# RWKV attention and a squared-ReLU FFN: chunk scores cut to 64-token halves, bonus sums moved to TensorE

## The chip, the cores and the metric

One Trainium2 chip, one core. The metric is device time in microseconds of one execution of the whole kernel, with all loads from and stores to device memory. All tensors are float32.

## What is computed

For each of 4 batches and 8 heads (head size 48) a linear recurrence runs over 768 tokens; its output, heads side by side, goes through a two-layer FFN with a squared ReLU.

```python
# r, k, v, w: [4, 8, 768, 48];  u: [8, 48];  w_in: [384, 2048];  w_out: [2048, 384]
for t in range(S):
    cur = einsum('bhd,bhe->bhde', u * k[t], v[t])
    y[t] = einsum('bhd,bhde->bhe', r[t], state + cur)
    state = w[t][..., None] * state + einsum('bhd,bhe->bhde', k[t], v[t])
x = y as [4 * 768, 384]
h = maximum(x @ w_in, 0)
out = (h * h) @ w_out
```

## The kernel before

**Chunks and units.** The 768 tokens are cut into 6 chunks of C = 128. A *unit* is one chunk of one batch, all 8 heads: 24 units, 4 per chunk. The 8 heads are handled as 4 pairs; a pair's two heads lie in partitions 0 to 47 and 64 to 111 (J = 64, HP = 112), so that products of one head use a 64x64 quarter of the TensorE array and four of them can be under way at once. Tokens are also cut into two halves of Q = 64.

**A unit, step by step** (`attention(c, b, rank)`):
- load w, k, r token-major into `st` (two units at a time) and v into `vt`; for chunk 0 TensorE transposes `st` into `pt` (L618, through PSUM), later chunks do it with a 32x32 VectorE transpose (L581) and small DMAs;
- `scan` (L630): running product of w along the tokens; `ln` (L637, L638): its inverse by Ln and Exp on ScalarE; `rt` (L641) and `kn` (L647, L648, L653): r times the decay before it, k over the decay up to it;
- the bonus term: r x k x u on GpSimd (L660, L662), a VectorE reduce per head and three small moves that put each token half where its block needs it (L666 to L669), then `diag` (L680, ScalarE): the 64x64 diagonal times the sum, eight times;
- `far` (L682, L683): a check of w's range, which would lead to a slow path at the end (not taken with these inputs);
- `scores` (L693): k against r, for the first 64 keys against all 128 queries, for the second 64 against the last 64; `mask` (L696) copies the causal part over the diagonal tile `m`;
- `past` (L715): the state `S` before the chunk against r, plus four transposes of k (L720), moved by ScalarE (L739); `mix` (L728): v against `m`, accumulated onto past; `outer` (L747): k^T v, added to the state by VectorE (L809), which GpSimd multiplies with the chunk's decay `Ec` (L812);
- `x` (L789, L790): the result in two parts, high and low, for the FFN's split products; a fourth pair goes through `x3` and six small DMAs.

Scores take two PSUM banks of a pool "a", past and mix take two. In chunk 0 there is no state; there the fourth pair's result is placed by a selection product (L755).

**FFN.** Per chunk 16 steps f of 128 hidden columns (`ffn`): nine products of 512 (or, in the first steps of chunks 0 and 1, 256) columns into a bank `hp` (L832), ReLU on ScalarE (L837), times itself on VectorE (L838), high part on ScalarE (L840), low part on VectorE (L841), and per batch three products of 384 columns into `ob` (L847). Weights arrive as raw words and are split into high and low parts by ScalarE, VectorE and GpSimd (L532 to L553) during chunk 0.

**Order of work.** Every step is handed to a planner (`Plan`) with an engine, an assumed cost, what it reads and writes, and a rank from a hand-kept table (`Ranks`). The planner plays the steps through with these costs, engine by engine, and writes each engine's instructions in the order of the assumed start times. A `mode` marks steps in 64x64 tiles: it assumes a price for entering and leaving them. Pools have a fixed number of places, and a step waits for a free one:

```python
P.pool("hp", hps)    # 2 PSUM banks
P.pool("a", pas)     # 2 PSUM banks
P.pool("m", ...)     # 7 tiles [128, 512]
```

Up to 110 us of planned time it puts filler transposes of the identity (L888) where it expects TensorE to be idle.

## Time and profile before

| | us |
|---|---|
| runs, median of 3 (range) | 546.95 (545.52 to 547.07) |
| the profiled execution | 545.76 |
| its span, first to last instruction | 543.9 |
| TensorE busy | 526.4 |
| VectorE busy | 367.1 |
| ScalarE busy | 281.8 |
| GpSimd busy | 101.4 |

In the page a busy time is the union of an engine's instructions. PE is TensorE's products, PEld its weight loads, DVE VectorE, ACT ScalarE, POOL GpSimd, SP the queue that issues most DMAs. A line such as L847 names the source line. Rows of the order of time give start, length, and how many instructions were merged; products overlap, so the distance to the next row's start says more than the length. f32 products of the attention appear as two instructions per call. TensorE's granted clock was 0.996 of full speed on the mean.

### The profile page before, as it was taken

What the parts mean: (1) busy time and instruction counts of PE and PEld (TensorE: products, weight loads), DVE (VectorE), ACT (ScalarE), POOL (GpSimd) and SP (SyncE); (2) the same over time, 40 slices, a digit from 0 to 9 for tenths busy, and PEclk for the clock granted to TensorE, in tenths of its full rate; (3) what the DMA queues carried; (4) which work ended last, traced back from release to release, by engine and by line L of the source; (5) the groups of instructions that cost most, each with busy time, mean ns of one, the idle gap of its engine ahead of it and who ended that gap; (6) DMA issues with size and microseconds to landing.
All of it is one profiled execution on the core that took longest, in us unless ns stands there. A gap on an engine that the chain in (4) does not pass through costs nothing.

```text
span 543.9 us, 12917 instructions
## 1 busy us (share of the span) xinstructions
PE 526.4 (97%) x5047; PEld 465.7 (86%) x5047; DVE 367.1 (67%) x770; ACT 281.8 (52%) x730; POOL 101.4 (19%) x121
## 2 busy tenths in 40 slices
PE   8899989999999999999999999999999999999995
PEld 8788978878999889988888888889888989899894
DVE  6889899989969596498859597875653233433331
ACT  3668568486664747356465757526433222432321
POOL 5344543144303021030301203020000000000000
PEclk9999999999999999999999999999999999999998
DMA  9979988666483745747256565644002000000001
GB/s 161 175 183 227 244 173 195 151 109 136 93 151 72 138 91 101 140 92 134 48 97 122 101 125 117 129 91 84 1 6 68 16 1 1 29 32 0 1 1 61
DMA packets 222978, 53.01 MB, mean 97 GB/s; under 512 B 212672, under 2 KB 217792, under 8 KB 222912
## 3 DMA queue, kind: packets, MB, share of 16 engines
q1 hardware_dynamic: 220016, 50.75, 46.6%
q10 hardware_dynamic: 2896, 1.38, 1.0%
q8 instruction: 42, 0.69, 0.6%
q14 instruction: 24, 0.20, 0.1%
HBM read 31.65 MB, written 4.72 MB: 67 GB/s over the span
## 4 chain that ended last, share of the span: by engine, by line
PE 77%; DMA 10%; DVE 4%; ACT 3%; SPq 3%; issue 1%; POOL 0%; ACTq 0%; DVEq 0%
PE hp L832 33%; PE ob L847 32%; DMA ri<-in_moe_w_in_dram 4%; DMA v<-in_v_dram 3%; PE a L693 3%; PE a L728 3%; DMA st<-in_w_dram 2%; PE a L715 2%; SPq L572 2%; PE a L720 1%; PE a L747 1%; ACT m L680 1%; SPq L605 1%; DVE g L841 1%; DVE pt L630 1%
## 5 line engine op out<-in xcount | busy, mean ns | idle before, releaser
L847 PE MATMUL ob<-wo,g 128*128 128x384 f32 x1152 | 223.4, 340 | 1.4 <-DVE g L841 1.4
L832 PE MATMUL hp<-x,wi 128*128 128x512 f32 (+1 forms) x1062 | 219.9, 355 | 3.4 <-DVE g L841 3.2
L847 PEld LDWEIGHTS ob<-wo,g 128*128 128x128 f32 x1152 | 198.9, 188 | 7.7 <-DVE g L841 2.2
L832 PEld LDWEIGHTS hp<-x,wi 128*128 128x128 f32 x1062 | 173.1, 188 | 32.8 <-DVE g L841 6.8
L838 DVE SCALAR_TENSOR_TENSOR hp<-hp,t 128x512 f32<-128x512 f32 (+1 forms) x118 | 69.8, 593 | 91.3 <-ACT t L837 90.8
L837 ACT ACTIVATE t<-hp 128x512 f32<-128x512 f32 (+1 forms) x118 | 61.1, 518 | 118.5 <-PE hp L832 64.2
L841 DVE TENSOR_TENSOR g<-hp,g 128x512 fp32r<-128x512 f32 (+1 forms) x118 | 68.9, 585 | 32.3 <-ACT g L840 31.6
L840 ACT CAST g<-hp 128x512 fp32r<-128x512 f32 (+1 forms) x118 | 59.7, 506 | 51.9 <-DVE hp L838 51.5
L680 ACT ACTIVATE m<-diag,beta 128x64 f32<-128x64 f32 x192 | 50.0, 340 | 11.6 <-DVE beta L668 7.3
L660 POOL TENSOR_TENSOR st<-st 128x384 f32<-128x384 f32 x24 | 24.3, 1017 | 65.6 <-DVE st L581 58.4
L630 DVE TENSOR_TENSOR_SCAN pt<-pt,zero 112x128 f32<-112x128 f32 x80 | 29.0, 412 | 1.7 <-DMA st<-in_w_dram 1.7
L790 DVE SCALAR_TENSOR_TENSOR x<-a,x 112x128 fp32r<-112x128 f32 (+2 forms) x68 | 20.2, 329 | 12.2 <-ACT x L789 10.9
L696 DVE COPY_PREDICATED m<-caus,a 128x384 f32<-128x384 uint8 x48 | 25.9, 584 | 3.1 <-PE a L693 2.9
L662 POOL TENSOR_TENSOR st<-st,un 128x384 f32<-128x384 f32 x24 | 27.3, 1141 | 1.6
L581 DVE STREAM_TRANSPOSE st<-st 128x1152 f32<-128x1152 f32 x20 | 27.0, 1361 | 0.0
L728 PEld LDWEIGHTS a<-m,v 64*48 64x48 f32 (+1 forms) x768 | 20.5, 126 | 7.3 <-issue 4.1
L637 ACT ACTIVATE m<-pt 112x512 f32<-112x512 f32 x24 | 15.2, 631 | 22.3 <-DVE pt L630 19.4
L693 PEld LDWEIGHTS a<-pt 48*64 48x64 f32 x768 | 19.2, 133 | 7.8 <-ACT m L680 1.6
L789 ACT ACTIVATE x<-a 112x128 fp32r<-112x128 f32 (+2 forms) x68 | 18.1, 313 | 14.1 <-PE a L747 7.0
L728 PE MATMUL a<-m,v 64*48 64x64 f32 (+3 forms) x768 | 24.8, 250 | 0.4 <-DVE m L696 0.4
L693 PE MATMUL a<-pt 48*64 48x128 f32 (+1 forms) x768 | 22.8, 250 | 1.4 <-DVE pt L653 1.4
L812 POOL TENSOR_TENSOR S<-S,Ec 112x192 f32<-112x192 f32 x16 | 8.1, 508 | 82.8 <-DVE S L809 82.8
(86 smaller groups left out, 441.8 us busy)
## 6 DMA issues: line engine op xcount, KB each, us to landing
pt<-st SPq DMA_DIRECT2D x120, 96.0 KB, 2.3
ro<-in_moe_w_out_dram SPq DMA_DIRECT2D x8, 768.0 KB, 7.4
v<-in_v_dram SPq DMA_DIRECT2D x88, 48.0 KB, 2.5
st<-in_w_dram SPq DMA_DIRECT2D x11, 384.0 KB, 4.4
st<-in_k_dram SPq DMA_DIRECT2D x11, 384.0 KB, 5.7
st<-in_r_dram SPq DMA_DIRECT2D x11, 384.0 KB, 5.7
out_dram<-q SPq DMA_DIRECT2D x20, 192.0 KB, 2.1
ri<-in_moe_w_in_dram SPq DMA_DIRECT2D x8, 384.0 KB, 6.4
```

The costliest lines, as they stand in the source:

```text
L581: V.transpose(out=zt[:, i].rearrange("a t p q i -> a t (p q) i"), in_=sv[:, :, i].rearrange("s t p q x -> s t (p q) x"))
L630: lambda p=p: V.tensor_tensor_scan(out=pt[:, 0, p], data0=src(0)[:, p], data1=zero.broadcast_to([HP, C]), initial=1.0, op0=ALU.mult, op1=A ...
L662: P.add("pool", 0.97, rank("rk"), lambda: G.tensor_tensor(out=rk(), in0=rk(), in1=un.rearrange("s (h d) -> s h d", d=D), op=ALU.mult), w=[ ...
L680: A.activation(Ms[j].tile[:, mo(p, y):mo(p, y) + Q], diag2, AF.Copy, scale=beta.tile[:, i:i + 1])
L693: T.matmul(mts[j].tile[q * Q:q * Q + Q, o:o + C - y * Q], kq[js, g:g + Q], pt[js, 1, 2 * q + p, y * Q:], start=True, stop=True, skip_group ...
L728: T.matmul(spot(p)[to:to + n + D, y * Q:], vt.tile[qs, o - n:o + D], Ms[j].tile[qs, mo(p, y):mo(p, y) + C - y * Q], start=(c == 0 and p == ...
L832: T.matmul(hp.tile[:, 0:n], wi[f][:, wl, kt], xT[:, kt, xl, xs], start=(m == 0), stop=(m == 3 * KT - 1))
L837: P.add("act", 0.49 if full else 0.28, rank("g"), lambda: A.activation(t(), h(), AF.Relu), r=[hp], w=[(g, 1)])
L838: P.add("dve", 0.6 if full else 0.33, rank("g"), lambda: V.scalar_tensor_tensor(out=h(), in0=h(), scalar=0.0, in1=t(), op0=ALU.max, op1=AL ...
L840: P.add("act", 0.48 if full else 0.26, rank("g"), lambda: A.copy(out=hi(), in_=h()), r=[hp], w=[(g, 0)])
L841: P.add("dve", 0.6 if full else 0.33, rank("g"), lambda: V.tensor_tensor(out=lo(), in0=h(), in1=hi().bitcast(F32), op=ALU.subtract), r=[hp ...
L847: T.matmul(obs[b][:, 0:DM], g.tile[0][:, gl, o:o + C], wo[f][:, wl], start=(f == 0 and m == 0), stop=(f == NF - 1 and m == 2))
```

## The change

- **Halves (chunks 1 to 5).** Scores are computed within each 64-token half only. The first half's k^T v is added to the state before the chunk, which gives a second state `S1` at mid-chunk; past then multiplies the first half's queries with `S` and the second half's with `S1`. `S2` is the state after the chunk before the decay.
- **Order of the groups.** From chunk 2 on, `advance(a, z)` puts past of one unit and outer of the next into one TensorE step, and mix of the one and scores of the next into another. In chunk 1 the units take these steps singly. Both banks of pool "a" are one tile `ab` and are always taken together. Outer alternates the banks against the column halves (`q ^ j`).
- **k's transposes** become a step of their own outside the 64x64 mode, into an `hp` bank, with one ScalarE copy.
- **Bonus sums (chunks 0 and 1).** VectorE multiplies r and k head-major; four small TensorE products with `ut` (u laid out by head, loaded by four small DMAs with 4-byte elements) sum over the head; ScalarE puts them in place. GpSimd's two passes, the reduce and the moves go for these units. In chunk 0 r is copied out of PSUM by ScalarE first.
- **FFN of chunk 0.** h x h is made on ScalarE as a Square of the ReLU's output.
- Mask, x and state steps work on both banks at once; one "m" tile less; all ranks and a few assumed costs differ.

The core of the diff (the rank tables left out):

```diff
-    LANES, RUNS, SLACK, START = 8, 2300, 1.0, 3.6
+    LANES, RUNS, SLACK, START = 8, 2300, 1.0, 4.0
...
-    pas = [ps_a.tile([128, 512], F32, name=f"a{i}") for i in range(2)]
+    ab = ps_a.tile([128, 1024], F32, name="ab")
+    pas = [ab[:, i * 512:i * 512 + 512] for i in range(2)]
...
+    ut = at.tile([HP, 2, 4], F32, name="ut")
+    G.memset(ut, 0.0)
+    for j in range(2):
+        for p in range(2):
+            nc.scalar.dma_start(out=ut[j * J:j * J + D, p]..., in_=u...)
...
+        if c < 2:   # attention: bonus sums of the first two chunks
+            P.add("dve", 0.59, rank("rk"), lambda: V.tensor_tensor(out=Ms[0]..., in0=turned(pt[:, 1]), in1=turned(src(2)), op=ALU.mult), ...)
...
+            def betas():
+                for g in range(4):
+                    T.matmul(bp.tile[:, g * 4:g * 4 + 4], Ms[0].tile[0:HP, g * C:g * C + C], ut[:, g // 2], start=(g == 0), stop=True, ...)
+            P.add("pe", 0.5, rank("beta"), betas, r=[Ms[0]], w=[bp])
+            def place_betas():
+                for q in range(2):
+                    A.copy(out=beta.tile[qs, 0:H]..., in_=bp.tile[qs, 0:16]...)
...
+            def turned_k():
+                for i, g in enumerate(range(0, 4, 3 - ys)):
+                    T.matmul(kp.tile[:, i * HP:i * HP + HP], kq[:, g * C:g * C + C], ident[0:HP, 0:HP], is_transpose=True, ...)
+            P.add("pe", 0.2 * ys, rank("ktp"), turned_k, r=KK, w=[kp])
+            P.add("act", 0.03 + 0.2 * ys, rank("kt"), lambda: A.copy(out=Kt..., in_=kp...), r=[kp], w=[Kt])
...
+            def outer(alone):     # 16 products of 48 columns (8 in the last chunk)
+                ...
+                T.matmul(ab[j * J:j * J + n, (q ^ j) * 512 + p * 2 * C + C + y * J:...], Kt..., vt..., start=(alone and p == 0 and y == 0), ...)
+            def inter():          # past: two states, 16 products of 64 columns
+                for h, t in enumerate((lambda: Ss[b], lambda: S1.tile)):
+                    ...
+                    T.matmul(ab[to:to + n + D, p * 2 * C + h * Q:...], t()[js, o - n:o + D], pt[js, 1, p, h * Q:h * Q + Q], ...)
+            def scores():         # 16 products of 64 columns
+            def mix():            # 16 products of 64 columns
...
+            def after_outer():
+                P.add("dve", 0.27, rank("S"), lambda: V.tensor_tensor(out=sv(S1.tile), in0=zone(0, D)[0:HP], in1=sv(Ss[b]), op=ALU.add), ...)
+                if not last:
+                    P.add("dve", 0.27, rank("S"), lambda: V.tensor_tensor(out=sv(S2.tile, 0), in0=zone(J, D)[0:HP], in1=sv(S1.tile), op=ALU.add), ...)
...
+    def advance(a, z):
+        if a: fns += [a["inter"]]
+        if z: fns += [lambda: z["outer"](not a)]
+        P.add("pe", cost, ..., lambda: group(fns), w=["Y", "dS", "scores"] + AB, mode=1, ...)
+        ...
+        if a: then += [a["mix"]]
+        if z: then += [z["scores"]]
+        P.add("pe", cost, ..., lambda: group(then), w=... + AB, mode=1, ...)
...
+        if c == 0:            # ffn
+            P.add("act", 0.49 if full else 0.28, rank("g"), lambda: A.activation(h(), t(), AF.Square), r=[(g, 1)], w=[hp])
+        else:
+            P.add("dve", ..., lambda: V.scalar_tensor_tensor(out=h(), in0=h(), scalar=0.0, in1=t(), op0=ALU.max, op1=ALU.mult), ...)
...
+            if c == 1:
+                advance(a, None)
+                advance(None, z)
+            else:
+                advance(a, z)
```

More of the change, by code (lines that the diff above doesn't have):

```diff
@@ L194 @@
 class Ranks:
[L196 removed]
+    NAMES = ('load', 'v', 'turn', 'scan', 'ln', 'rk', 'rt', 'kn', 'beta', 'diag', 'far', 'mt', 'mask', 'mix', 'x', 'kt', 'dS', 'S', 'z', 'pt', 'ktp', 'past', 'x3', 'send')
     UNITS = (
[24 rows of a table removed]
[L222 to L224 removed]
[24 rows of a table added]
+    )
@@ new lines, in moves @@
+        def moves(outs, between):
+            for nm, sl, y, hi, lo, k1, c1, c2 in outs:
+                P.add("act", c1, rank(nm), lambda y=y, hi=hi: A.activation(hi(), y(), AF.Copy, scale=-1.0), r=[sl], w=[k1 + ("hi",), (sl, "bank")], after=freed)
+            between()
+            for nm, sl, y, hi, lo, k1, c1, c2 in outs:
+                P.add("dve", c2, rank(nm), lambda y=y, hi=hi, lo=lo: V.scalar_tensor_tensor(
+                    out=lo(), in0=y(), scalar=-1.0, in1=hi().bitcast(F32), op0=ALU.mult, op1=ALU.subtract), r=[sl, k1 + ("hi",)], w=[k1 + ("lo",), (sl, "bank")])
@@ L801, in attention @@
[L801 to L812 removed]
+        ly = Slot("ly")
@@ new lines, in between @@
+        def between():
+            for q in range(KT):
+                T.matmul(spot(TILES[q]), sel[:, q], ly.tile, start=(q in (0, 2)), stop=False, skip_group_check=True)
+            across()
+            part(TILES)
+        P.add("pe", 0.34, rank("mix"), lambda: part([SPLIT]), r=[*VK, *Ms], w=[(far_yb, 3)], mode=3, claim=[yb, ly, Kt])
+        P.add("act", 0.14, rank("mix"), lambda: A.copy(out=ly.tile, in_=spot(SPLIT)[0:HP]), r=[(far_yb, 3)], w=[ly])
+        P.add("pe", 1.82, rank("mix"), between, r=[*VK, *Ms, *KK, ly], w=[*both_yb, *KW], mode=3, more=14 if b == 1 else 0)
@@ new lines, in attention, with state @@
+        P.add("pe", 0.46, rank("dS"), outer, r=[*VK, (Kt, 0), (Kt, 1)], w=[*both_yb, *KW], mode=3, more=-10 if b == 1 else 0)
+        for i, t in enumerate(both_yb):
+            def state(i=i, t=t):
+                ps = slice(2 * i, 2 * i + 2)
+                V.tensor_tensor(out=Sd[:, ps], in0=t.tile[0:HP, 2 * C:2 * C + 2 * D].rearrange("a (p e) -> a p e", p=2), in1=Eb()[:, ps], op=ALU.mult)
+            P.add("dve", 0.165, rank("S"), state, r=[(t, "dS"), Ec], w=[("S", b)])
+    stages, opened = [], []
@@ new lines @@
+    AB = [Slot("a") for _ in range(2)]
+    def advance(a, z):
+        fns, r, w, cost = [], [], ["Y", "dS", "scores"], 0.0
+        after = [] if a else opened or [s for s in P.steps if any(x.pool == "a" for x in s.slots)]
+        if a:
+            fns, r, cost = fns + [a["inter"]], r + a["r2"], cost + 0.45
+        if z:
+            fns, r, cost = fns + [lambda: z["outer"](not a)], r + z["r1"], cost + z["outer_cost"]
+        group = lambda fns: [fn() for fn in fns]
+        P.add("pe", cost, a["rank"]("past") if a else z["rank"]("dS"), lambda: group(fns), r=r, w=w + AB, mode=1, claim=[a["x3"]] if a else [], after=after)
+        if a:
+            a["after_inter"]()
+        if z:
+            z["after_outer"]()
+        else:
+            P.add("act", 0.06, a["rank"]("S"), lambda: A.copy(out=nothing, in_=ab.rearrange("a (k x) -> a k x", k=2)[0:HP, :, 0]), r=["Y"], w=["past"])
+        then, r, cost = [], [], 0.0
+        if a:
+            then, r, cost = then + [a["mix"]], r + a["r4"] + ([] if z else ["past"]), cost + 0.45
+        if z:
+            then, r, cost = then + [z["scores"]], r + z["r3"], cost + 0.45
+        P.add("pe", cost, a["rank"]("mix") if a else z["rank"]("mt"), lambda: group(then), r=r, w=w + AB, mode=1, claim=[z["M"]] if z else [])
+        mask = z["after_scores"] if z else lambda: None
+        if a:
+            opened[:] = a["after_mix"](mask)
+        else:
+            mask()
```

505 lines of the change are left out of this document (271 added, 234 removed), and 48 rows, old and new, of the table UNITS.

## The prediction

> **What bounds the kernel now.** I read the page first (busy shares, chain), then the windows by phase, then the order of time on TensorE in a steady stretch. Page lines, the windows of all engines, and the windows of the filler transposes of L888 alone:
>
> ```profile
> span 543.9 us, 12917 instructions
> ...
> PE 526.4 (97%) x5047; PEld 465.7 (86%) x5047; DVE 367.1 (67%) x770; ACT 281.8 (52%) x730; POOL 101.4 (19%) x121
> ...
> PE 77%; DMA 10%; DVE 4%; ACT 3%; SPq 3%; issue 1%; POOL 0%; ACTq 0%; DVEq 0%
> ...
> 0.00:41.42 41.42, 36.39 (x424) 33.18 (x424) 33.38 (x84) 23.79 (x66) 18.49 (x35) 1.00 0.95 174
> 41.42:133.69 92.27, 88.05 (x850) 77.42 (x848) 84.63 (x160) 63.42 (x152) 38.22 (x28) 1.00 0.79 174
> 133.69:400.00 266.31, 264.33 (x2966) 231.96 (x2966) 203.14 (x457) 150.78 (x426) 44.66 (x59) 1.00 0.53 101
> 400.00:537.62 137.62, 137.62 (x813) 123.09 (x811) 45.94 (x72) 42.96 (x87) 0.00 (x0) 1.00 0.05 17
> ...
> 0.00:41.42 41.42, 24.21 (x172) 21.24 (x172) 1.00 0.95 174
> 41.42:133.69 92.27, 1.69 (x11) 1.31 (x11) 1.00 0.79 174
> ```
>
> The first number after a stretch is its length, the second TensorE's busy time. Four phases. Until 41.42 us no FFN product runs: 24.21 of TensorE's 36.39 us are fillers, DMA's share is 0.95. From 41.42 to 133.69 (FFN of chunk 0, attention of chunk 1) TensorE has 92.27 - 88.05 + 1.69 = 5.9 us of slack. From 133.69 to 400 it has 2.0, after that none; the last 6.3 us are the way out. So after 41 us time is worth what TensorE's instruction stream is worth, and VectorE, at 84.63 of 92.27, is the engine that could bind in phase two. The granted clock is 1.00 in all four.
>
> **One unit of attention on TensorE.** FFN alone, late in the run, then one whole unit (chunks 1 to 4) between FFN products:
>
> ```profile
> 470.47 3.31 PE L847 MATMUL ob<-wo,g 128*128 128x384 f32 x18
> 473.62 4.32 PE L832 MATMUL hp<-x,wi 128*128 128x512 f32 x18
> 477.77 2.44 PE L847 MATMUL ob<-wo,g 128*128 128x384 f32 x13
> ...
> 240.37 0.90 PE L693 MATMUL a<-pt 48*64 48x128 f32 x32
> 241.20 2.88 PE L847 MATMUL ob<-wo,g 128*128 128x384 f32 x15
> 244.01 0.67 PE L715 MATMUL a<-pt,S 48*64 48x128 f32 x16
> 244.61 0.60 PE L720 MATMUL a<-ident,pt 112*128 112x112 f32 x4
> 244.98 2.31 PE L832 MATMUL hp<-x,wi 128*128 128x512 f32 x9
> 247.22 0.90 PE L728 MATMUL a<-m,v 64*64 64x128 f32 x32
> 247.92 0.65 PE L747 MATMUL a<-v,m 64*48 64x48 f32 x32
> 248.50 2.31 PE L832 MATMUL hp<-x,wi 128*128 128x512 f32 x9
> 250.65 1.22 PE L847 MATMUL ob<-wo,g 128*128 128x384 f32 x6
> ```
>
> I use start to next start, since busy times overlap. FFN: 3.15/18 = 0.175 us per second product, 4.15/18 = 0.2306 per first one. The unit: 240.37 to 250.65 is 10.28 us, less 15 x 0.175 and 18 x 0.2306, leaves 3.50 us for one unit: scores 0.83, past 0.60 and its transposes 0.37, mix 0.70, outer 0.58, and 0.43 that the FFN products next to the three groups take longer than alone (0.14 a group). Scores and mix have the same shapes; scores end in FFN, mix runs on into outer, so leaving the 64x64 tiling costs 0.83 - 0.70 = 0.13 inside a group. A group thus costs 0.27 beside its products (bounds: 0.14, the neighbours alone, to 0.43, if all of a unit's excess went with one group).
>
> Scores of that unit by shape (mean ns of one instruction in the first column after the bar's busy time):
>
> ```profile
> L693 PE MATMUL a<-pt 48*64 48x128 f32 x16 | 0.8, 283 | 0.0
> L693 PE MATMUL a<-pt 48*64 48x64 f32 x16 | 0.6, 217 | 0.0
> ```
>
> 32 instructions of about 250 ns pass in 0.83 us, so they run some four abreast on four quarter tiles, and a 64-column one is 66 ns shorter than a 128-column one.
>
> **The change on TensorE.** All f32 products count double in the records (16 calls, 32 instructions).
> - Chunks 2 to 4. Scores and mix lose their cross-half blocks: each becomes 32 instructions of 64 columns. The state at mid-chunk (S1) carries that part, so past becomes 32 of 64 instead of 16 of 128. Price of 32 x 64 from mix: 0.70 less four fours that get 0.066 shorter = 0.44 (by columns, two thirds, 0.47; bounds 0.35, half, and 0.70, if instructions and not columns set the price). Outer keeps 32 x 48, at 0.58 - 0.13 = 0.45 (below: 0.33 = 0.44 x 48/64, because its banks are now crossed; nothing shows that, so I take the row). Transposes stand alone in untiled mode: 0.37. Groups: two instead of three, since past of one unit and outer of the next go together, and mix with the next scores. After: 0.37 + 0.45 + 3 x 0.44 + 2 x 0.27 = 2.68 against 3.50, so 0.82 saved, times 12 units = **-9.8**.
> - Chunk 1 doesn't pair units: four groups, and the bonus products: 4 calls, 8 instructions with 128-column weights and 4 columns. Nearest rows are the six products of L755 and the transposes:
>
> ```profile
> 24.82 0.83 PE L755 MATMUL a<-ly,sel 112*128 112x128 f32 x6
> 25.49 0.55 PE L720 MATMUL a<-ident,pt 112*128 112x112 f32 x4
> ```
>
> L755 to the next start is 0.67/6 = 0.11 each, the transposes 0.09; 8 of them 0.7 (bounds 0.3, a third of that for 4 columns, to 0.9). After: 2.68 + 2 x 0.27 + 0.7 = 3.92, 0.42 more, times 4 = **+1.7**.
> - Last chunk. Rows before:
>
> ```profile
> 401.87 0.67 PE L715 MATMUL a<-pt,S 48*64 48x128 f32 x16
> 402.47 0.79 PE L847 MATMUL ob<-wo,g 128*128 128x384 f32 x3
> 403.19 0.90 PE L728 MATMUL a<-m,v 64*64 64x128 f32 x32
> 404.02 3.42 PE L847 MATMUL ob<-wo,g 128*128 128x384 f32 x18
> ```
>
> 0.60 + 0.83 + scores 0.83 + 0.43 = 2.69. After: two transposes 0.19, half an outer 0.22, 3 x 0.44, two groups 0.54 = 2.27. Times 4 = **-1.7**.
> - Chunk 0 keeps its products and gains four times the bonus product, 2.8 us in all; those before 41 us come out of fillers, so I take a quarter: **+0.7** (0 to 2.8).
>
> **The other engines.** They are worth only what they do to phases one and two.
>
> ```profile
> L838 DVE SCALAR_TENSOR_TENSOR hp<-hp,t 128x512 f32<-128x512 f32 x74 | 51.4, 695 | 82.2 <-ACT t L837 81.7
> L838 DVE SCALAR_TENSOR_TENSOR hp<-hp,t 128x256 f32<-128x256 f32 x44 | 18.4, 422 | 9.1 <-ACT t L837 9.1
> L653 DVE TENSOR_TENSOR pt<-pt,m 112x512 f32<-112x512 f32 x20 | 13.9, 697 | 0.1
> L666 DVE TENSOR_REDUCE beta<-st 128x8 f32<-128x384 f32 x24 | 12.9, 539 | 1.9 <-POOL st L662 1.9
> L837 ACT ACTIVATE t<-hp 128x512 f32<-128x512 f32 x74 | 44.2, 598 | 97.9 <-PE hp L832 51.4 <-PE ob L847 45.7
> L837 ACT ACTIVATE t<-hp 128x256 f32<-128x256 f32 x44 | 16.9, 384 | 20.6 <-PE hp L832 12.9 <-PE ob L847 7.5
> L660 POOL TENSOR_TENSOR st<-st 128x384 f32<-128x384 f32 x24 | 24.3, 1017 | 65.6 <-DVE st L581 58.4
> ...
> 41.42 1.34 PE L832 MATMUL hp<-x,wi 128*128 128x256 f32 x9
> ...
> 74.20 1.34 PE L832 MATMUL hp<-x,wi 128*128 128x256 f32 x9 [1.02 <-DVE g L841]
> ...
> 79.81 0.98 PE L847 MATMUL ob<-wo,g 128*128 128x384 f32 x4 [1.36 <-DVE g L841]
> ```
>
> Chunk 0's squares, 12 half and 10 full, leave VectorE (12 x 0.422 + 10 x 0.695 = 12.0 us) for ScalarE (12 x 0.384 + 10 x 0.598 = 10.6). In eight units the reduce (0.539, and three small moves behind it) gives way to one product r x k of about 0.70 (L653's form), roughly even on VectorE, and 16 GpSimd passes of about 1 us go. New on ScalarE: in chunk 0 a copy of r's 512 columns (about 0.59 each), two small copies of the sums per unit. ScalarE has 63.42 of 92.27 in phase two, so there is room; what queues behind the squares there are the weights' casts and the diagonals. VectorE's queue gets 12 us lighter where two of its late results alone held TensorE 1.02 and 1.36 us: of the 5.9 us slack I take 1.8 (bounds: 3.6 gained, 3 lost if ScalarE becomes the late one): **-1.8**. In phase one four tiny DMAs of 4-byte elements on ScalarE's queue stand beside loads that fill DMA (share 0.95), and the first unit's sums no longer wait for GpSimd; planned ranks of all loads differ, which no row prices. I take **-0.5** (-5 to +6, the first FFN product at 36 to 47 us). SP's queue carries the same transfers in a new order. In chunks 2 to 5 VectorE trades two masks for one, and two half-size state adds for two whole ones; GpSimd keeps the decay: nothing, hidden by 92 us a chunk of FFN products; uncovered, the S1 add sits between a unit's two groups and would cost its own half microsecond.
>
> New waits: the transposes and chunk 1's sums now take one of the two hp banks (24 times, each about 0.37 plus a ScalarE copy, about 1.2 us), and both attention banks now form one resource, so scores wait for the state adds, the next past for mask and moves. Behind a waiting product on TensorE's queue stands all FFN work. An FFN step holds its bank for less than the 8.3 us that two steps take, so most fit; I take 0.08 each: **+2.0** (0 to 12, half a microsecond each).
>
> Sum: -9.8 + 1.7 - 1.7 + 0.7 - 1.8 - 0.5 + 2.0 = -9.4. The profiled execution took 545.76 us (543.9 of span and 1.9 around), 1.2 below the median of the runs shown, 546.95. So 545.76 - 9.4 = **536.4 us**.
>
> **A rule against a row.** Past sends both row halves of the array into one bank at a time, and so do the new past and the crossed outer. L715 took 0.60 for 16 x 128: two thirds of the columns of scores (0.70 x 2/3 = 0.47) and 0.13 for leaving; one row half after the other would be 1.07. The Trainium skill ("TensorEngine Tiling (Array Packing)", Gotcha 1: PSUM Pressure) says that different row tiles cannot access the same PSUM bank at once. By that rule past and outer would double; by the row they don't, and the sum goes by the row.
>
> **Rivals.**
> 1. *Instructions, not columns, set the price.* The 32 x 64 groups then cost 0.70 each: a unit 3.46 (no gain), chunk 1 +4.8, last chunk +1.4; with the other terms 545.76 + 6.1 = 551.9. For it: outer, with 48 columns, takes hardly less than mix with 96 on average. Against it: 217 against 283 ns by shape. It decides from 0.65 per group on. Chance 0.04. The Trainium skill ("TensorE: Matmul & The Clock Gate", "Wait — 56ns, not 53.3ns?") gives a floor of about 25 ns from start to start; the trace disagrees for quarter tiles, with 0.58/32 = 18 ns in outer.
> 2. *Row halves serialise on a bank* in the crossed outer and the short past: 0.89 more in 16 units and 0.66 in 4, 16.9 us, 553. Against it: L715's 0.60. Chance 0.02.
> 3. *The first FFN product comes late* (41.42 to 47 or later) by the new load order and the extra work on ScalarE: 541 to 547. For it: DMA's share of 0.95. Against it: fewer GpSimd and VectorE passes in that chain. It undoes the gain from 9.4 us on. Chance 0.10.
> 4. *hp banks*: each of the 24 new users stalls TensorE by 0.3 to 0.5 us: 542 to 547. For it: both banks are in use nearly always. Against it: 2.0 us of idle time in 266 us with the same step chain. Chance 0.08.
> 5. *More is gained*: the start 4 us sooner and most of phase two's slack gone: 526 to 530.5. Chance 0.08.
>
> The forecast, 530.5 to 540.5, has 0.68. The range 530.5 to 543.5 adds the nearer halves of rivals 3 and 4. A change within 0.3% (1.6 us) can't be told from none here. Faster: 0.68 + 0.08 and the near parts of 3 and 4, 0.84; same 0.06; slower 0.10 (rivals 1, 2 and the far ends of 3 and 4).
>
> **What would show it.** Right: in the profile after, mix and scores in one run of 64 instructions of 64 columns in about 1.0 us to the next FFN start, past and outer likewise; TensorE's slack between 134 and 400 us still near 2; the FFN rows unchanged at 0.175 and 0.23; first FFN product at 38 to 43 us; all of the gain between 134 and 420 us. Wrong: groups of 64 instructions near 1.4 us; idle time before hp or the transposes put down to ScalarE's Kt copy; first FFN product past 45; VectorE no lighter because it now waits for ScalarE's square before the low part.

## The result, and the profile after

The changed kernel took 568.5 us (median of 4 runs, 567.1 to 569.0), the kernel before 546.2 in the same session: ratio 1.040, 95% interval 1.038 to 1.043. The forecast was 536.4, and slower had been given 0.10. The profiled execution took 568.97 us.

Its span is 567.3 us (543.9 before). The lines give the busy time of each engine in four stretches. The stretches end where the same piece of work starts in both kernels: the first, the 25th and the 67th FFN step, and TensorE's last product. The second fence counts the filler transposes alone, in the first two stretches. After:

```profile
0.00:50.36 50.36, 38.40 (x424) 34.15 (x424) 30.95 (x71) 24.58 (x59) 13.90 (x38) 0.93 0.91 167
50.36:163.20 112.84, 104.78 (x1104) 93.39 (x1101) 82.47 (x136) 80.78 (x203) 34.86 (x31) 0.98 0.61 139
163.20:315.20 152.00, 142.84 (x1843) 129.21 (x1844) 114.54 (x257) 89.20 (x248) 32.64 (x59) 0.98 0.58 110
315.20:560.80 245.60, 245.57 (x2166) 218.58 (x2165) 125.21 (x227) 101.22 (x224) 15.18 (x22) 1.00 0.23 47
```
```profile
0.00:50.36 50.36, 22.23 (x151) 19.17 (x151) 0.93 0.91 167
50.36:163.20 112.84, 8.95 (x60) 8.26 (x60) 0.98 0.61 139
```

Before, the same stretches of work (the first, to 41.42 us, stands in the prediction; fillers take 24.21 us in the first and 1.69 in the second):

```profile
41.42:137.40 95.98, 91.76 (x904) 80.93 (x902) 88.30 (x166) 65.31 (x156) 39.52 (x28) 1.00 0.79 175
137.40:288.20 150.80, 148.83 (x1822) 132.93 (x1822) 114.69 (x276) 88.94 (x267) 27.93 (x39) 1.00 0.57 107
288.20:537.60 249.40, 249.39 (x1904) 218.61 (x1902) 130.72 (x247) 102.90 (x242) 15.42 (x19) 1.00 0.24 49
```

Columns: length, then busy time of TensorE, its weight loads, VectorE, ScalarE, GpSimd, then the granted clock. Stretch by stretch the changed kernel is 8.9, 16.9 and 1.2 us longer and 3.8 shorter. Take TensorE's busy time without fillers: 526.37 - 25.90 = 500.5 before, 531.59 - 31.18 = 500.4 after. Its own work takes as long as before. Length less busy time plus fillers, the time in which TensorE had nothing to do, went from 29.2 + 5.9 + 2.0 + 0.0 = 37.1 to 34.2 + 17.0 + 9.2 + 0.0 = 60.4: all 23 us are there.

The attention itself got shorter, but by less than forecast. A unit's five pieces in the fourth stretch:

```profile
321.50 0.55 PE L741 MATMUL hp<-ident,pt 112*128 112x112 f32 x4
321.82 1.29 PE L973 MATMUL ob<-wo,g 128*128 128x384 f32 x6
323.04 0.69 PE L766 MATMUL ab<-pt,S 48*64 48x64 f32 x32
323.53 0.66 PE L755 MATMUL ab<-v,m 64*48 64x48 f32 x32
324.12 2.36 PE L955 MATMUL hp<-x,wi 128*128 128x512 f32 x9
326.41 0.69 PE L785 MATMUL ab<-m,v 64*64 64x64 f32 x32
326.90 0.67 PE L775 MATMUL ab<-pt 48*64 48x64 f32 x32
327.50 0.80 PE L973 MATMUL ob<-wo,g 128*128 128x384 f32 x3
328.15 2.24 PE L955 MATMUL hp<-x,wi 128*128 128x512 f32 x9
```

From start to next start: transposes 0.32, past 0.49, outer 0.59, mix 0.49, scores 0.60, in all 2.49. The FFN products behind them take longer than alone, as they did before: 1.22 instead of 1.05 behind the transposes, 2.29 instead of 2.08 behind outer, 0.65 instead of 0.53 behind scores. With these, as the prediction counts, the unit takes 6.65 us from 321.50 to 328.15 less nine products at 0.175 and nine at 0.2306, so 3.00 against 2.68 forecast and 3.50 before. The pair mix and scores passes in 1.09 us, as said.

The waits lie at the start and in the second and third stretch. TensorE and ScalarE's queue at the start, after:

```profile
9.07 3.98 ACTq L505 DMA_DIRECT2D ut<-in_u_dram  x4
13.09 0.63 ACT L646 ACTIVATE m<-pt 112x512 f32<-112x512 f32 x1 [9.91 <-DMA ut<-in_u_dram]
```
```profile
15.86 1.87 PE L682 MATMUL ab<-ut,m 112*128 112x4 f32 x8 [4.76 <-POOL ut L506]
```

ScalarE first gets rid of the four little ut loads, which takes it 3.98 us. Issuing one takes 0.32 to 0.44 us of that; the rest is waiting, as the row of the last load alone shows:

```profile
12.73 0.32 ACTq L505 DMA_DIRECT2D ut<-in_u_dram  x1
```

In the trace every load uses one of eight semaphores, and waits for the landing of the load that used it before. For the first, third and fourth ut load that is a load of `st` on SP's queue, which landed at 8.99, 10.18 and 12.71 us; the ut loads start at 9.07, 10.20 and 12.73. Only then come the first unit's Ln and Exp, and the last ut load lands at 15.43: TensorE waits 4.76 us for ut, which GpSimd has to negate first, ahead of the first bonus product. In the stretch behind it the clock halves (12 to 20 us, by windows of 4 us):

```profile
12.00:16.00 4.00, 0.14 (x1) 0.83 0.69 164
16.00:20.00 4.00, 4.00 (x20) 0.50 0.96 252
```

Then, between the second and third FFN step, and at one place in the third stretch:

```profile
52.73 1.32 PE L955 MATMUL hp<-x,wi 128*128 128x256 f32 x9
58.13 5.35 PE L1019 MATMUL ab<-ident 128*128 128x128 f32 x32 [4.08 <-DVE pt L670]
63.24 1.31 PE L955 MATMUL hp<-x,wi 128*128 128x256 f32 x9
...
258.66 4.18 PE L955 MATMUL hp<-x,wi 128*128 128x512 f32 x9 [3.38 <-DMA x<-x]
```

Fillers, which are there to keep TensorE busy, themselves wait 4.08 us for VectorE and then hold the third FFN step back by another 5.1. Ahead of 258.66 the six little moves of the fourth pair's result (from 253.60, 4.82 us) stand behind eight moves of `pt` (from 247.24, 5.52 us) on SP's queue; the product that waited then runs at half clock (4.18 us instead of 2.2).

### The profile page after: what moved, and what is told of

It reads as the page before. It is cut to its first block, busy times and chain, and to the rows that moved or that the text cites. A ratio compares the mean times of both kernels' runs of the same rounds, so it can differ in the third digit from the quotient of the medians.

```text
span 567.3 us, 13809 instructions
## 1 busy us (share of the span) xinstructions
PE 531.6 (94%) x5531; PEld 475.3 (84%) x5531; DVE 353.2 (62%) x689; ACT 296.6 (52%) x733; POOL 96.6 (17%) x147
## 4 chain that ended last, share of the span: by engine, by line
PE 76%; DVE 7%; SPq 5%; DMA 5%; ACT 4%; issue 2%; ACTq 0%; DVEq 0%; POOL 0%; POOLq 0%
PE hp L955 32%; PE ob L973 32%; SPq L600 3%; PE ab L785 2%; DMA v<-in_v_dram 2%; PE ab L766 2%; PE ab L1019 1%; PE ab L755 1%; DVE st L590 1%; PE ab L775 1%; PE hp L741 1%; SPq L581 1%; DMA st<-in_r_dram 1%; DVE g L967 1%; DMA ro<-in_moe_w_out_dram 1%
## 5 line engine op out<-in xcount | busy, mean ns | idle before, releaser
L964 DVE SCALAR_TENSOR_TENSOR hp<-hp,t 128x512 f32<-128x512 f32 (+1 forms) x96 | 58.1, 606 | 88.0 <-ACT t L960 87.0
L967 DVE TENSOR_TENSOR g<-hp,g 128x512 fp32r<-128x512 f32 (+1 forms) x118 | 68.8, 585 | 43.0 <-ACT g L966 42.7
L736 ACT ACTIVATE m<-diag,beta 128x64 f32<-128x64 f32 x160 | 40.3, 337 | 2.2 <-DVE beta L700 2.1
L1019 PE MATMUL ab<-ident 128*128 128x128 f32 x140 | 21.8, 315 | 8.6 <-DVE pt L670 4.8
L718 ACT ACTIVATE x<-ab 112x384 fp32r<-112x384 f32 (+3 forms) x48 | 16.5, 374 | 24.2 <-PE ab L775 13.7
L1019 PEld LDWEIGHTS ab<-ident 128*128 128x128 f32 x140 | 19.7, 167 | 9.3 <-ACT g L966 4.3
L562 POOL TENSOR_TENSOR wi<-q,wi 128x768 fp32r<-128x768 f32 x8 | 17.9, 2238 | 53.2 <-ACT wi L561 37.0
L691 POOL TENSOR_TENSOR st<-st 128x384 f32<-128x384 f32 x16 | 16.6, 1038 | 52.7 <-DVE st L590 39.8
L721 DVE SCALAR_TENSOR_TENSOR x<-ab,x 112x384 fp32r<-112x384 f32 (+3 forms) x48 | 18.4, 401 | 10.7 <-ACT m L896 5.5
L804 DVE COPY_PREDICATED m<-caus,ab 128x512 f32<-128x512 uint8 x20 | 14.7, 737 | 12.6 <-ACT x L718 11.2
L662 POOL COPY Ec<-pt 64x4 f32<-64x4 f32 x20 | 8.0, 402 | 80.7 <-DVE pt L639 78.1
L562 POOL TENSOR_TENSOR wo<-q,wo 128x768 fp32r<-128x768 f32 x8 | 15.9, 1992 | 21.5 <-ACT wo L561 21.0
```

Source lines behind the costliest of these rows:

```text
L562: P.add("pool", 1.78, rank, lambda q=q, tt=tt: G.tensor_tensor(out=tt[:, 1], in0=q.tile, in1=tt[:, 0].bitcast(F32), op=ALU.subtract), r=[q ...
L721: P.add("dve", c2, rank(nm), lambda y=y, hi=hi, lo=lo: V.scalar_tensor_tensor(out=lo(), in0=y(), scalar=-1.0, in1=hi().bitcast(F32), op0=A ...
L736: A.activation(M.tile[:, o:o + Q], diag2, AF.Copy, scale=beta.tile[:, i:i + 1])
L964: P.add("dve", 0.6 if full else 0.33, rank("g"), lambda: V.scalar_tensor_tensor(out=h(), in0=h(), scalar=0.0, in1=t(), op0=ALU.max, op1=AL ...
L967: P.add("dve", 0.6 if full else 0.33, rank("g"), lambda: V.tensor_tensor(out=lo(), in0=h(), in1=hi().bitcast(F32), op=ALU.subtract), r=[hp ...
L1019: P.filler = lambda bank: T.transpose(out=bank[:, 0:128], in_=ident, identity=ident)
```

## The experiments

Four suspects: the ut load, the tile `ab` (two banks under one name), the new work itself in a full first chunk, and the order of the steps. The first four runs take the load and the fillers.

**ut as a constant** (`ut_const`; the bonus sums then use -0.1 for u).

```diff
-    G.memset(ut, 0.0)
-    for j in range(2): ...4 x nc.scalar.dma_start(out=ut..., in_=u...)
-    G.tensor_scalar(out=ut, in0=ut, scalar1=-1.0, ...)
+    G.memset(ut, -0.1)
```

> The changed kernel with ut filled by a constant instead of four small DMAs of 4-byte elements (so the bonus sums of chunks 0 and 1 are not those of u); nothing else differs, the written order is the same. Theory A (the late ut load holds ScalarE's queue until 13.1 us and TensorE's until 15.9 us, and all of chunk 0 starts late): ScalarE's first Ln at about 9 us, first FFN product at 40 to 43 us instead of 50.4, total 549 to 554 us. Theory B (the first chunk is late because ScalarE has too much to do, squares and copies included): the first Ln comes earlier, but the first FFN product stays past 46 us, total 562 to 567. Theory C (the attention groups of later chunks cost more than forecast): under 2 us gained.

Measured 565.1 us, ratio 1.034 (1.030 to 1.038); first FFN product at 45.72. That start lies between the two theories, and the time in the range of Theory B: 3.4 us less than with the load, and not the 14 or more of Theory A.

**ut loaded first** (`ut_early`): its memset on VectorE, its four loads ahead of everything on ScalarE's queue, `un` behind it.

```diff
+    V.memset(ut, 0.0)                        # ahead of the memsets of st0
+    for j in range(2): ...4 x nc.scalar.dma_start(out=ut..., in_=u...)
...
+    G.tensor_scalar(out=ut, in0=ut, scalar1=-1.0, ...)
     nc.scalar.dma_start(out=un, ...)         # moved behind it
```

> The changed kernel with the four ut DMAs issued first on ScalarE's queue, after a VectorE memset, instead of behind the u load and GpSimd's work on it; same numbers, same order otherwise. Theory A: most of the gain of the constant ut, so the first FFN product at 40 to 45 us, total 550 to 558. Theory B: 562 to 568. If the four DMAs are slow wherever they stand (3.98 us to issue), the first v loads come later by 4 us and half of the gain is lost.

Measured 565.7 us, ratio 1.036 (1.032 to 1.040), the same as without a load: the first FFN product where Theory A has it, the time where B has it. TensorE's fillers and third FFN step:

```profile
52.73 6.02 PE L1019 MATMUL ab<-ident 128*128 128x128 f32 x32 [4.09 <-DVE pt L670]
58.50 1.31 PE L955 MATMUL hp<-x,wi 128*128 128x256 f32 x9
```

The first FFN product comes 5.4 us sooner, at 44.95, but of that only 2.8 us arrive at the end; the wait of the fillers is as long as it was.

**The load in the kernel before** (`before_ut`): the same memset, loads and negation, whose result nothing reads.

```diff
     G.tensor_scalar(out=un, ...)
+    ut = at.tile([HP, 2, 4], F32, name="ut")
+    G.memset(ut, 0.0)
+    for j in range(2): ...4 x nc.scalar.dma_start(out=ut..., in_=u...)
+    G.tensor_scalar(out=ut, in0=ut, scalar1=-1.0, ...)
```

> The kernel before with the changed kernel's four ut DMAs, its memset and its negation added at the same place and used by nothing. Theory A in its narrow form (ScalarE's queue is held by these DMAs whoever reads ut): ScalarE's first Ln at about 13 us instead of 8.9, total 550 to 556. If the stall is TensorE's and GpSimd's wait for ut alone: 546 to 548. Theory B and C: 546 to 548.

Measured 553.3 us, ratio 1.013 (1.008 to 1.018): 7 us for a tensor of 1.5 KB. The time is that of Theory A, but ScalarE's wait is not the whole cause. ScalarE and GpSimd in it, then GpSimd in the kernel before:

```profile
6.20 4.40 ACTq L502 DMA_DIRECT2D ut<-in_u_dram  x4
10.65 0.63 ACT L643 ACTIVATE m<-pt 112x512 f32<-112x512 f32 x1 [8.05 <-DMA ut<-in_u_dram]
...
14.60 0.24 POOL L503 TENSOR_SCALAR ut<-ut 112x8 f32<-112x8 f32 x1 [8.39 <-DMA ut<-in_u_dram]
14.93 0.99 POOL L666 TENSOR_TENSOR st<-st 128x384 f32<-128x384 f32 x1
```
```profile
9.24 1.04 POOL L660 TENSOR_TENSOR st<-st 128x384 f32<-128x384 f32 x1 [0.18 <-PE ob L618]
```

ScalarE's first Ln comes at 10.65 instead of 8.91 (Theory A had said 13). GpSimd is held longer: the negation of ut waits for the landing until 14.60, and the first unit's bonus passes behind it start 5.7 us later than before. TensorE then waits 7.51 us for that unit's diagonals, to 22.02, where its scores had started at 16.08, and the clock stands at half from 18.2 to 28.4 us. So the price is what stands behind the load in two queues, the one that issues it and the one that first uses it, and the clock that falls in the wait. With ut first the same four are issued in the idle start, in 2.03 us, done before any work arrives:

```profile
0.97 2.03 ACTq L457 DMA_DIRECT2D ut<-in_u_dram  x4
```

**No fillers** (`no_fill`).

```diff
-    P.filler = lambda bank: T.transpose(out=bank[:, 0:128], in_=ident, identity=ident)
+    P.filler = None
```

> The changed kernel without filler transposes; the order of all other work is the same. Theory A with fillers as amplifier (a filler count fixed for planned idle time is burned after the work is already late, as in 58.1 to 63.2 us, where 32 fillers stand ahead of an FFN product): first FFN product at 46 to 48 us, total 558 to 563. Rival (the fillers hold the granted clock, and it falls below 1.00 in the first 60 us without them): chunk 0's products take up to twice as long, total 568 to 576.

Measured 571.8 us, ratio 1.045 (1.039 to 1.050). The wait of the fillers is gone with them, but the granted clock is lower, here from the first FFN step to the seventh:

```profile
52.46:87.10 34.64, 29.49 (x326) 26.70 (x323) 21.75 (x37) 21.50 (x63) 8.28 (x4) 0.80 0.88 188
```

0.80 where the changed kernel has 0.95 between the same steps. Time and clock are those that the rival gave, and the first FFN product comes later than with fillers, at 52.46. This run can't say what the fillers' wait costs. Nor is the clock shown to be the whole reason: two of its four runs had a mean clock of 0.986 and 0.987, above the changed kernel's 0.979 to 0.983, and took 568.1 and 571.7 us.

**Fillers into hp only** (`fill_hp`, on top of ut first).

```diff
-                bank = next((x[1] for p in ("a", "hp") for x in self.pools.get(p, ()) if x[0] <= idle), None)
+                bank = next((x[1] for p in ("hp",) for x in self.pools.get(p, ()) if x[0] <= idle), None)
```

> The early-ut kernel with one more edit: the warm-up products of TensorE are written only into the hp banks, never into a half of the joined tile ab; order and all other work as in the early-ut kernel (565.7 us, its first FFN product at 44.95, its third at 58.50, its seventh at 82.0). Theory 1 (a warm-up product into one half of ab waits for VectorE's readers of the other half, and the 32 products behind that wait then push the FFN product by 6 us): the stall before the third FFN product goes, first FFN product 42 to 44, third 48 to 53. If that wait is what the first chunk loses, the seventh comes at 74 to 77 and the time is 557 to 561. Theory 2 (the fourth unit's chain through the two halves of ab sets the first chunk's end, whatever the warm-up does, as the kernel with no warm-up products hints: its seventh FFN product came as late against the first as with them): the third product comes early, but the seventh still at 79 to 82, time 562 to 566.

Measured 562.2 us, ratio 1.029 (1.026 to 1.033). The third FFN product comes at 52.62, as Theory 1 has it, but it now waits itself, 3.40 us for VectorE, and runs at half clock (2.15 us to the next start instead of 1.18); the seventh comes at 77.7, between the two theories, and the time lies in the range of Theory 2. The clock blurs it: it stood at half from 11.8 to 25.4 us here, against 13.1 to 16.6 with ut first alone. The fillers' wait was part of the loss, and VectorE's results still came late. The next two runs look for the reason in the tile.

**One name for two banks, in the kernel before** (`before_ab`). The cleanest of these: order, instructions and data are those of before.

```diff
-    pas = [ps_a.tile([128, 512], F32, name=f"a{i}") for i in range(2)]
+    ab = ps_a.tile([128, 1024], F32, name="ab")
+    pas = [ab[:, i * 512:i * 512 + 512] for i in range(2)]
```

> The kernel before, with one edit: its two PSUM tiles of the a pool are made one tile of two banks and used as its two halves, as the changed kernel has it; order, instructions and data the same. Theory 1 (waits follow the tile's name, so work in one half waits for readers of the other): TensorE's waits on VectorE and ScalarE ahead of 60 us grow, first FFN product 42.5 to 46 (41.42 before), time 548 to 552. Theory 2 (only the bytes touched count): first FFN product 41.2 to 41.7, time within 0.3% of before, 544.5 to 547.5.

Measured 552.6 us, ratio 1.012 (1.010 to 1.015): Theory 1 and a little above its range, 7.1 us by the medians of that session, at a clock as high as before (0.995 to 0.998). TensorE's waits in it (us in total, times, longest), then waits of the kernel before:

```profile
PE ab L889 <- DVE pt L654: 1.9, 1, 1.9
PE ab L748 <- DVE x L791: 1.8, 2, 1.3
PE ab L716 <- DVE m L697: 1.2, 1, 1.2
```
```profile
PE a L693 <- DVE pt L653: 1.4, 1, 1.4
PE a L715 <- DVE m L696: 0.7, 1, 0.7
PE a L747 <- DVE x L790: 0.3, 1, 0.3
```

The wait of outer (L748, before L747) for x and that of past (L716, before L715) for the mask grow; before, no filler waits for VectorE, and the 1.4 us ahead of scores are 0.2 here. Work in one bank waits for readers of the other. These are the program's waits, not the memory's: the kernel before uses the same two banks without them. The Trainium skill ("PSUM — Partial Sum Buffer", PSUM bank collisions raise a hardware error) asks for guards by bank and quadrant, and says that accesses to different banks run clean.

**Two tiles in the first chunk** (`split_a`, on top of ut first): the pool holds two tiles until the second chunk's first group opens, then `ab` is made of the same banks.

```diff
-    ab = ps_a.tile([128, 1024], F32, name="ab")
-    pas = [ab[:, i * 512:i * 512 + 512] for i in range(2)]
+    pas = [ps_a.tile([128, 512], F32, name=f"a{i}") for i in range(2)]
+    class Joined:              # stands for ab: at its first use it closes
+        ...                    # the pool of pas and makes the tile of 1024
+    ab = Joined()
```

> The early-ut kernel (565.7 us) with one edit: in the first chunk the two PSUM banks of the a pool are two tiles again, as in the kernel before; the joined tile ab is made of the same two banks when the first group of the second chunk opens. Order, warm-up products and work are the same. Theory 1 (work in one half of ab waits for readers of the other half, which cost the kernel before 7 us when its two tiles were joined, some 4 of them ahead of 60 us): the wait of 4.1 us ahead of the third FFN product goes, that product comes at 49 to 54 instead of 58.5, and the time is 559 to 563. Theory 2 (the order of the steps through the two halves sets it: a unit's bonus product needs one of the two halves and stands between two units' other work): third product earlier, seventh still 79 to 82, time 563.5 to 566.

Measured 557.7 us, ratio 1.021 (1.018 to 1.024): 8.0 us less than with ut first alone, more than Theory 1 gave; the seventh FFN step comes at 72.3, so Theory 2 is out. The fillers no longer wait, and the third FFN product comes at 49.30:

```profile
45.84 3.66 PE L1035 MATMUL a<-ident 128*128 128x128 f32 x32
```

Part of the 8.0 us comes through the clock: here it stands at full speed for the first 226 us, while with ut first alone it fell to half at 13.1 and at 50.7 us.

**Another order** (`reorder`). What is left, 12 us, can be the new work or the order of the steps, which the rank tables decide. They were searched anew (simulated annealing on the ranks, with the kernel's own planner as the measure), everything else as in the last kernel but for two assumed costs and the fillers' bank:

```diff
-    IDLE = (110.0, 4.0, 0.3, 0.12)
+    IDLE = (110.0, 4.0, 0.3, 0.135)
-            P.add("pe", 0.5, rank("beta"), betas, ...)
+            P.add("pe", 0.95, rank("beta"), betas, ...)
...      all numbers of UNITS, LOAD, SPLIT and FFN
```

> The last kernel (ut early, two tiles in the first chunk) with the same work in another order: the numbers of the rank tables, by which the kernel's planner picks the next step, are searched anew; the planner's costs of the bonus product (0.95) and of a warm-up product (0.135) are set to what the traces show, and warm-up products go to the hp banks only. The planner's own end for this order is 533.6, against 543.7 for the order of the changed kernel and 536.6 for that of before, where the chip took 545.8. Theory 1 (the change's own work is not what loses the time, the order of its steps is): 541 to 548, first FFN product 36 to 40, TensorE's warm-up products and idle time together 30 to 42 us instead of 57.6. Theory 2 (the new work loses it, in waits that no order mends: bonus sums through PSUM and ScalarE ahead of every unit, squares on a full ScalarE, the joined tile): 553 or more.

Measured 546.6 us, ratio 1.002 (1.001 to 1.003): 11.0 us less by the order and the two small edits, as fast as before. Theory 1. (Fillers became fewer with it, 114 instead of 211.) Its first two stretches, to the same FFN steps as above, last 39.95 and 111.55 us, with TensorE busy for 31.55 and 105.72, of which fillers 15.28 and 3.12. That leaves 23.7 and 9.0 us without work, against 34.2 and 17.0 in the changed kernel. But the clock has fallen in them, to 0.87 and 0.97.

**Only the halves** (`halves`): the bonus sums and the squares go back, ut with them.

```diff
-        if c < 2:          # VectorE product, TensorE sums
+        if False:          # every chunk: GpSimd, reduce, moves
...
-        if c == 0:         # ffn: Square on ScalarE
+        if False:
...      all numbers of UNITS, LOAD, SPLIT and FFN
```

> Only the first part of the change: scores inside halves with two states per unit. The bonus sums stay on GpSimd and VectorE in every chunk, the squares on VectorE, and ut is not loaded; two tiles in the first chunk; ranks searched anew for as long as those of the last kernel (the planner's own end is 536.8). Theory A (the halves carry all the gain, the other two parts are paid for by the first chunk): at or below the reordered kernel, 540 to 546. Theory B (the relief of VectorE and GpSimd in the first two chunks is worth what the planner gives it): 2 to 6 us above the reordered kernel, 545 to 552.

Measured 551.5 us, ratio 1.009 (1.006 to 1.012), 4.9 us above the reordered kernel: Theory B, if two searches are a fair comparison. They need not be, so both were searched again.

**Two more orders** (`reorder2`, `halves2`). Edits: the numbers of the rank tables, and fillers into either free bank of the first chunk again.

> All three parts of the change (ut early, two tiles in the first chunk) in a third order. The rank tables of the reordered kernel (546.6 us) are searched on, now for an order that also ends early when transfers land later and VectorE and ScalarE take 2 to 6% longer than planned, with the order held; warm-up products go to either free bank again. The planner's own end is 529.5 (533.6 for the reordered kernel, 536.6 for before). Theory 1 (what was left after the first search are waits from an order with no room for late results: TensorE's first bonus products, the scores behind them, the stall of 3.9 us on VectorE's product): 537 to 543, below before, warm-up products and idle time together 24 to 31 us instead of 33.5. Theory 2 (the new work in the first two chunks sets a floor that no order lowers): 544.5 to 548, no better than the first search.

> Only the first part of the change (scores inside halves), bonus sums and squares as in the kernel before, two tiles in the first chunk, ranks searched in the same way and as long; the planner's own end is 535.4. Theory A (the halves carry the gain; with a fair order the other two parts cost more than they give): 535 to 540 and at or below the twice reordered kernel. Theory B (the bonus products and the squares on ScalarE relieve VectorE and GpSimd in the first two chunks by more than their 8 us of TensorE): 3 to 8 us above the twice reordered kernel, 541 to 548.

Measured 543.1 us, ratio 0.994 (0.991 to 0.997), and 544.9 us, ratio 0.998 (0.997 to 1.000). The first lies on the edge of Theory 1's range, the difference of 1.8 us between the two fits neither A nor B. The 12 runs of the first spread from 539.4 to 545.9 and go with the granted clock: five at 0.989 to 0.992 took 539.4 to 540.7, six at 0.976 to 0.980 took 543.7 to 545.9 (one at 0.986, 542.5). Same program, same work: 5 us by the clock. Where it falls, in windows of 4 us (length, TensorE's busy time, clock, DMA) and in rows:

```profile
40.00:44.00 4.00, 2.91 (x18) 0.84 1.29 179
44.00:48.00 4.00, 4.00 (x21) 0.50 1.16 204
48.00:52.00 4.00, 4.00 (x47) 0.81 1.01 246
```
```profile
41.34 0.66 PE L643 MATMUL a<-ident,st 128*128 128x128 f32 x4 [0.56 <-ACT beta L704]
42.53 2.14 PE L971 MATMUL hp<-x,wi 128*128 128x256 f32 x9 [0.53 <-DVE g L983]
44.47 1.70 PE L698 MATMUL a<-ut,m 112*128 112x4 f32 x8
46.03 2.27 PE L971 MATMUL hp<-x,wi 128*128 128x256 f32 x9
```

Two waits of half a microsecond, together 1.09 us in 4, and the next FFN products take 1.94 and 2.07 us to the next start instead of 1.18. The halves' runs, all at 0.988 to 0.995, took 543.0 to 546.6: at like clocks the whole change is about 5 us better than the halves alone.

**Does the search help before as well, and is the rest the clock?** (`before_reorder`: the kernel before, rank numbers alone; `reorder3`: the twice reordered kernel, rank numbers alone.)

> The kernel before with nothing changed but the numbers of its rank tables, searched in the same way and about as long as those of the twice reordered changed kernel (543.1 us): for an order that ends early also when transfers land late and VectorE and ScalarE are slower than planned. The planner's own end is 535.8 (536.6 for its own order). Theory 1 (the change is worth something of its own: 12 us of attention on TensorE less 8 us of bonus products): this order gains little, 544 to 547, and the twice reordered changed kernel stays below it. Theory 2 (the gain of the twice reordered kernel came from the search and not from the change): 539 to 543.

> The twice reordered changed kernel (543.1 us; its runs go from 539.4 at a granted clock of 0.992 to 545.9 at 0.976) in a fourth order. The search now also counts TensorE's products behind about 1 us of idle time within 4 us at half speed for 4 us, as the windows at 42 to 48 us show it. The planner's own end is 531.9 (529.5 for the twice reordered kernel), so without the clock it should be 2 us later. Theory 1 (the clock takes the rest): mean granted clock 0.988 or more in the profile, 538 to 542. Theory 2 (the clock falls by other rules than that, or the waits are elsewhere): clock 0.975 to 0.985, 543 to 547.

Measured 546.2 us, ratio 0.999 (0.997 to 1.001): Theory 1 by the median. But its 12 runs fall apart by the clock as well: five at 0.988 to 0.991 took 543.3 to 544.1 us, seven at 0.983 and 0.984 took 546.2 to 547.2. At its better clock the new order gains some 2 us on the old one (545.7), which its worse clock takes away again. And 539.6 us for the last order (537.8 to 541.2), ratio 0.990 (0.987 to 0.992), profiled at a clock of 0.992: Theory 1 again. The order planned 2 us later is 3.5 us faster. It is 1% faster than before, but the kernel before was never searched against the clock: by searches of the same kind the difference is 3.1 us (543.1 against 546.2), and about 4 us in the runs at a clock near 0.99 (539.4 to 540.7 against 543.3 to 544.1). Its first three stretches (fillers: 17.48 and 1.42 us in the first two; in the fourth, 245.56 us, TensorE is never without work):

```profile
0.00:36.23 36.23, 31.51 (x378) 28.52 (x378) 25.91 (x65) 22.54 (x56) 11.16 (x36) 0.95 1.11 198
36.23:138.15 101.92, 98.11 (x989) 87.34 (x989) 85.70 (x146) 82.75 (x206) 38.63 (x32) 0.98 0.83 165
138.15:284.78 146.63, 142.61 (x1912) 128.26 (x1911) 111.83 (x254) 88.04 (x248) 29.46 (x55) 1.00 0.67 113
```
Time without work: 22.2 + 5.2 + 4.0 + 0.0 = 31.5 us (37.1 before, 60.4 in the changed kernel). TensorE's own work: 517.79 - 18.90 = 498.9 us (500.5 before).

In sum, by medians: 568.5, ut first 565.7, two tiles in the first chunk 557.7, three times another order 546.6, 543.1, 539.6. Taken off in this sequence, the 22 us above before are 3 of a load that came late, 8 of two banks under one name, and 11 of an order of steps (with the fillers' bank and two assumed costs). In another sequence the parts may differ. With these removed and the order searched against the clock the changed kernel is 6 us below the one before; what of that is the change and what the search against the clock is not separated, and like searches give 3 to 4.

## Why the prediction was wrong

Its forecast of 536.4 is 32 us off for the kernel as it was changed. The last order comes within 3.2 us of it, but by luck: the sum had 9.1 of its 9.4 us from TensorE's own work, while there TensorE's own work is 1.6 us shorter than before and 5.6 us are waits that went. Step by step, with the profiled executions:

- **The unit on TensorE, -9.8 and -1.7: right in kind, too large.** 3.00 us against 2.68, so 0.50 saved a unit and not 0.82, about 6 us in 12 units. The groups' own rows came near the forecast (2.49 for 2.40); what was mis-sized is what FFN products lose beside them, 0.51 instead of 0.28, above all behind the transposes, which stand alone now and were given no such cost. Summed over TensorE's rows, start to next start without waits, the attention of chunks 1 to 5 took 60.3 us before and 51.1 after, 9.2 less; the terms said 12.6 without the bonus products, neighbours included. One reading behind the price of 0.44 was wrong as well: 32 instructions of 250 ns in 0.83 us are nearly ten under way at once (8.0 / 0.83), not four. The price was near all the same, 0.49. Rivals 1 and 2 are out: 32 products of 64 columns take 0.49 us, the crossed outer 0.59.
- **The bonus product, 0.7 each: too small.** 0.97 on the mean of eight (the first, at half clock, took 1.87). All eight make 7.7 us of TensorE time instead of 5.6, and the first chunk's were booked as +0.7, since they would come out of fillers. They did, but a bonus product stands in a chain: it needs one of the two attention banks, then a ScalarE copy, the diagonals, and only then the unit's scores. The prediction had them as load and not as a link.
- **Phase one, -0.5 with -5 to +6: the step that failed first.** The first FFN product came at 50.36, past the bound of 47. The four tiny loads were listed, "on ScalarE's queue", but what they wait for and what stood behind them was not: landings of `st` ahead of them, the first Ln and the first bonus product behind. That is 5.4 us of it (44.95 with ut first), of which 2.8 reach the end. Another 2.6 go with the joined tile: with two tiles the first FFN product comes at 42.31.
- **Phase two, -1.8 with -3.6 to +3: wrong in sign.** 5.9 us without work became 17.0. VectorE got lighter, as said (88.3 to 82.5 us in that stretch), but its results came no sooner. ScalarE went from 65.3 to 80.8, and VectorE's low parts now wait 11.0 us for ScalarE's high parts, where they waited 2.3. The prediction had named that, "3 lost if ScalarE becomes the late one", as the bad end of its range. Besides, fillers waited for VectorE through the joined tile. How the 11 us more without work divide between the two no run shows. VectorE's waits in that stretch (us in total, times, longest), after and before:

```profile
DVE g L967 <- ACT g L966: 11.0, 12, 2.3
```
```profile
DVE g L841 <- ACT g L840: 2.3, 4, 0.9
```

- **New waits, +2.0 with 0 to 12: too small.** From 2.0 to 9.2 us in the third stretch, 7.2. The transposes into the hp banks wait 1.1 us in all. The rest is FFN products that wait for VectorE's low parts before they get their hp bank (5.1 there), and once for six moves on SP's queue (3.4). Whether the transposes' use of the banks lengthens the waits for the low parts, as the term had it, no run shows. In the whole run these are 6.9 us in ten waits, against 3.2 in five before.
- **What had no term.** The prediction saw that both banks "now form one resource" and priced it for the units of chunks 1 to 4, where the program takes both at once anyway. The same line joins them for the first chunk and for the fillers, where before two pieces of work had one bank each: 7.1 us in the kernel before, 8.0 here, a part of it by the clock. And "planned ranks of all loads differ, which no row prices" was put at nothing by a range of 11 us on phase one, while the order of all steps was worth 11 to 18 us.
- **The clock** stood at 1.00 in every row before, and so the sum had no term for it. In the changed kernel it is 0.93, 0.98 and 0.98 in the first three stretches. By the trace 8.7 us of TensorE's own work ran at half clock, so some 4.3 us are lost there (an estimate: half of it). These and the 7.7 us of bonus products take up the 9.2 that the attention gave and what little changed elsewhere, and TensorE's own work came out even, 500.4.

Rival 3 (first FFN product late) named the right place, with 0.10 and a price of 541 to 547; the cause it gave, load order and work on ScalarE, was a part of it. The main fault is one of accounting: every term was priced by its engine's time, and hardly any by what a late result holds up: 51 of the 60 us without work lie in the first 163 us, in chains over several engines, two banks and the queues.

What stays open: whether the kernel before gains as well from a search against the clock; how the 5 us between the whole change and the halves alone divide between bonus products and squares, since each structure needs an order of its own; and what the joined tile still costs in chunks 1 to 5, where mask, x and state steps work on both banks at once.

## What to carry to other kernels

- A tile that spans two banks makes waits for both: joining tiles for the sake of wider instructions in one stage costs every other stage that used them apart. Join them where the stage begins.
- A load of a kilobyte is priced by what stands behind it, in the queue that issues it and in that of the engine that first uses it. Put it where both are idle.
- When a change moves the step list of a kernel whose order is planned, compare it only with an order planned anew, and look anew at the old kernel in the same way; and judge an order by the idle moments it leaves ahead of the point where TensorE is saturated, not by its planned end alone.

## What the runs showed of the hardware

- The granted clock falls to 0.50 after little idle time, and in the traces for 3.4 us or two, three or four times that: 3.4 at 59.0 us and 6.8 at 14.7 and 257.0 in the changed kernel, 10.2 with the load in the kernel before, 13.7 with fillers into hp only. At 42 us above it is 6.8, from 42.7 to 49.5. The Trainium skill ("TensorE: Matmul & The Clock Gate", Part 1: The HAM clock gate) speaks of an idle window of about 3.4 us. In the changed kernel the fall at 12 us agrees (0.14 us busy in 4); the one at 42 us above does not, where two waits of 0.56 and 0.53 us were enough. Nor is it a fixed sum: the kernel before was busy for 2.51 of the 4 us from 12 to 16 and kept 1.00, as it did in the next 4:

```profile
12.00:16.00 4.00, 2.51 (x21) 1.00 1.03 235
```

- One load of single 4-byte elements takes 0.40 to 0.59 us to issue at the start of the kernel and 0.32 to 0.44 later. Four hold ScalarE for 2.0 us at the start, and for 4.0 to 4.4 us where two of them also wait for the landings of earlier loads.
- A product of 4 columns against 128-column weights takes 0.12 us an instruction (7.74 us for 64, eight of them at half clock), no less than one of 128 columns (0.11 in the selection products of the prediction's row). Its columns are not what it costs.
